# Block-sparse attention with a top-1 mixture of experts: exponentials, turned copies and gathered tokens in another order

## Chip, cores and metric

The kernel runs on one core of a Trainium2 chip. The metric is device time in microseconds (us), the median of several executions; lower is better. TensorE (PE, with its weight loads PEld), VectorE (DVE), ScalarE (ACT), GpSimd (POOL) and SyncE (SP, which here only issues DMAs) each run a queue of their own.

## The reference

```python
def _attn_ref(q, k, v, sampled_blocks):            # B=4, H=8, S=768, D=64
    scores = np.matmul(q, k.transpose(0, 1, 3, 2)) / np.sqrt(D)
    # blocks of 32: own block and both neighbours, the first and the last block
    # for all (their rows and their columns), 3 sampled blocks for each query block
    scores = np.where(mask, scores, -1000000000.0)
    attn = np.exp(scores - np.max(scores, axis=-1, keepdims=True))
    attn = attn / (np.sum(attn, axis=-1, keepdims=True) + 1e-09)
    return np.matmul(attn, v)

def _moe_ref(x, w_gate, w_output_gate, w1, w2):    # x: 3072 tokens x 512, 8 experts, FF 1024
    logits = x @ w_gate
    e_idx = np.argmax(logits, axis=1)
    gate_w = softmax(logits)[np.arange(N), e_idx]
    eom = 1.0 / (1.0 + np.exp(-(x @ w_output_gate)))
    for e in range(E):
        mask = e_idx == e
        h = np.maximum(x[mask] @ w1[e], 0.0)
        out[mask] = gate_w[mask, None] * eom[mask, e, None] * (h @ w2[e])
```

The tokens x are the attention's output, with the heads side by side.

## The kernel before

**Attention.** The work is cut into 52 pieces in a fixed order, and the loop at L1231 to L1265 runs one step for each, with three pieces in flight: in step n the scores of piece n (`now.pS`), the transposes of piece n-1 (`last.pT`) and the product with the values of piece n-2 (`before.pO`). The heads and batches form two groups (`bp`), and each has first four `Dense` pieces (query blocks 0 and 23, which see all 768 keys) and then 22 `Sparse` ones. So steps 0 to 3 and 26 to 29 make dense scores, and steps 1 to 4 and 27 to 30 turn the dense exponentials.

A dense piece does this: `pS` (L530) makes the scores in sixteen matmuls, which alternate between the two score banks S; `dM` (L538) takes the two maxima mx0d and mx1d on VectorE; `aE` (L546) makes four tiles of exponentials on ScalarE, P00d and P01d from the first bank, P10d and P11d from the second; `pT` (L553) turns each of the four by three transposes on TensorE (`turned`, L430, tiles T0d to T3d, for which there are two buffers) and copies the result out, T0d and T1d on ScalarE (L433), T2d and T3d on VectorE (L435); `pO` (L563) multiplies by the values, and `fin` (L442 to L444) divides. The next piece's scores overwrite both score banks, so they need the exponentials of the piece before.

In the program, in a step whose last piece is dense, `before.pO`, `last.pT(0)`, `now.dM` and `last.pT(1)` come first, and `now.aE` later, behind the work of other parts that the step holds (`mixed`, `run`). Each engine takes its instructions in the order in which the program records them.

**Experts.** Tokens are routed while the attention goes on (`route_a` to `route_d`; a scatter for each group of token tiles at the steps in SCATTER; `choose` picks five early units of work, u = 0 to 4, as soon as a group of tokens is known), and the rest is planned from step 26 + 31 on (`plan`). A unit is one expert with up to 256 tokens, and it is worked off in eight main steps, one for each piece of 512 KB of the expert's weights. FIRST = 31: main step 0 is step 31 of the loop. For each piece: `load_w` (L897, on SP), the high half of the weights in f16 on ScalarE (`w_h`, L976), the low half on VectorE (`w_l`, L980), twelve matmuls `p_h` (L994), relu into two halves (`h_h` L1007, `h_l` L1013) and the second product `p_y` (L1026); at the unit's end the scaled output (`y_o`, L1037) and its scatter to the result in HBM (`store_y`, L1044, on POOL).

The tokens of a unit come in four operations: `load_t` (L889, SP: the unit's part of the table of token numbers), `load_x` (L918, POOL: gathers of 128 tokens), `x_s` (L928 on ScalarE and L929 on VectorE: high and low half) and `x_t` (L943, DMA transposes on SP, for units from 6 on; units up to 5 are transposed by TensorE, L948, with a copy by ScalarE, L949). The planner (`program`, L1155) gives each operation a main step and a rank; `t = 8 * u` is the step of the unit's first piece.

Of the kernel before, what the change touches and what calls it, by code (L numbers as in the profile page):

```python
# [33 lines left out]
NE = 5  # L34
# [14 lines left out]


EARLY = {1: (0,), 2: (1, 2), 3: (3,), 4: (4,)}
EARLY_T = 27, 36, 38, 47, 52
EARLY_X = (28, 29), (37, 37), (39, 40), (48, 49), (53, 54)

SCATTER = {0: (18, 19, 20, 21), 1: (26, 26, 27, 27), 2: (34, 34, 35, 36), 3: (44, 45, 46, 47), 4: (50, 51, 52)}
OF = {u: g for g, us in EARLY.items() for u in us}

SX = 64.0
# [8 lines left out]
FIRST = PER + ND + 1  # L67
# [7 lines left out]
PEX = tuple(range(NE + 1))  # L75
# [21 lines left out]
def tile_kernel(ctx, tc, q, k, v, sampled, wg, wcat, out):  # L97
# [416 lines left out]
    class Dense:  # L514
# [34 lines left out]
        def pT(self, b):  # L549
            if b == 0:  # L550
                self.t = []
            for n in (2 * b, 2 * b + 1):
                self.t.append(turned(f"{n}" + self.name, self.p[n], 384, ("act", "dve")[b]))  # L553

        def pO(self):
            bp, u = self.k
# [505 lines left out]
    def at(n, rank, f, *a):  # L1062

        hooks.setdefault((n, rank), []).append((f, a))
# [31 lines left out]
    for bp in range(2):  # L1096
# [18 lines left out]
        for n, i in enumerate(tiles):  # L1115
# [7 lines left out]
            for g, (a, e) in enumerate(RG):  # L1123
                if e == tt + 1:
# [17 lines left out]
                    if g in EARLY:  # L1142
# [4 lines left out]
                        for u in EARLY[g]:  # L1147
                            at(t0 + 6, 3, load_r, u)
                            at(EARLY_T[u], 3, load_t, u)
                            for m in range(2):  # L1150
                                at(EARLY_X[u][m], 3, load_x, 2 * u + m)

    done = set()

    def program(n0, n1):  # L1155

        prog = {}

        def do(step, rank, f, a):
            u = NFC if f in (load_w, w_h, w_l, p_h, p_y) else NFC // 2 if f in (h_h, h_l) else 2 if f in (x_t, x_l, load_x, store_y) else 1  # L1160
            if n0 * u <= a < n1 * u and (f, a) not in done:
                done.add((f, a))
                prog.setdefault(step, []).append((rank, len(prog[step]) if step in prog else 0, f, a))

        for i in range(len(PLAN[1])):
            do(PLAN[0] + i, 11.5, plan, i)
        end = PLAN[0] + len(PLAN[1])
        for u in range(NUNIT):
            t = 8 * u
            yl = 2 if u < NOWN else 4  # L1170
            if u >= NE:
                later = end + u - NE
                do(max(t - 26, later), 0, load_g, u)
                do(max(t - 18, later), 0.5, load_t, u)
                for m in range(2):
                    do(max(t - 13, later + 1), 1, load_x, 2 * u + m)
                do(max(t - 7, later + 2), 13, x_s, u)
            for m in range(2):
                x = max(t - 2 + m, EARLY_X[u][m] + 1 - FIRST) if u < NE else t - 2 if u in PEX else t - 5
                do(x, 15, x_t, 2 * u + m)  # L1180
                do(x + 1 if u < NE else x, 3 if u < NE else 16, x_l, 2 * u + m)
            do(t + 8 + yl, 4 if u < NOWN else 12, y_o, u)
            for m in range(2):
                do(t + 8 + yl + 1 + (m if u < NOWN else 0), 13, store_y, 2 * u + m)
        for n in range(NP):
            e = n < NFC * NOWN
            lead, yl = (2, 2) if e else (3, 4)
            do(n - lead, 6, w_h, n)
            do(n - lead, 7, w_l, n)
            u, j = n // 8, n % 8  # L1190
            if e:

                do(max(n - 5, (-3, 5, 5, 15)[u]), 0.6, load_w, n)
            elif u < NE:
                do(n - 10, 0.6, load_w, n)
            else:
                do(max(n - 24 - lead + 1, end + u - NE, (30 + j // 2, 34 + j // 2)[u - NE] if u < NE + 2 else 0), 0.6, load_w, n)
            do(n, 8, p_h, n)
            do(n + yl, 9, p_y, n)
            if n % 2 == 1:  # L1200
                do(n if e else n + 1, 10, h_h, n // 2)
                do(n + 1, 2 if e else 11, h_l, n // 2)
        return prog
# [27 lines left out]
    for step in range(max(s for s, _ in hooks) + 1):  # L1231
        cur[0] = step
        now, last, before = unit(step), unit(step - 1), unit(step - 2)
        if now:
            now.pS()

        if isinstance(last, Dense):
            if before:
                before.pO()
            last.pT(0)  # L1240
            now.dM()
            last.pT(1)
        mixed(step, 0, 7)
        run(step, 0)
        if before and not isinstance(last, Dense):
            before.pO()
        if now and not isinstance(last, Dense):
            now.dM()
        run(step, 1)
        if before:  # L1250
            before.fin()

        if isinstance(now, Dense):
            now.aE()
        run(step, 2)
        mixed(step, 7, 9)
        if isinstance(now, Sparse) and step >= ONE_S:
            now.aE()
        if isinstance(last, Sparse):
            last.pT()  # L1260
        if isinstance(now, Sparse) and step < ONE_S:
            now.aE()
        mixed(step, 9, 99)
        for rank in (3, 4, 5):
            run(step, rank)  # L1265
# [64 lines left out]
```

## Time and profile before

| | |
|---|---|
| three executions | 608.76, 610.13, 615.25 us; median 610.13 |
| the profiled execution | 613.64 us, of it 611.8 in the span that the trace covers |
| mean granted clock of TensorE | 0.957 |
| busy share: PE, PEld, DVE, ACT, POOL | 89%, 62%, 63%, 56%, 38% |
| DMA | 136.28 MB, mean 223 GB/s |

A busy time is summed over the span, so it hides that the stages have different limits: the dense steps lie at 10 to 37 us and at 140 to 183 us, the sparse steps between and behind them, and expert work alone from about 320 us. A matmul line of the trace stands for a group of matmuls; "[0.41 <-ACT P01d L546]" at a line's end is the time that the engine was idle before it, and what ended it. [...]

### The profile page before, as it was taken

What the parts mean: (1) busy time and instruction counts of PE and PEld (TensorE: products, weight loads), DVE (VectorE), ACT (ScalarE), POOL (GpSimd) and SP (SyncE); (2) the same over time, 40 slices, a digit from 0 to 9 for tenths busy, and PEclk for the clock granted to TensorE, in tenths of its full rate; (3) what the DMA queues carried; (4) which work ended last, traced back from release to release, by engine and by line L of the source; (5) the groups of instructions that cost most, each with busy time, mean ns of one, the idle gap of its engine ahead of it and who ended that gap; (6) DMA issues with size and microseconds to landing.
All of it is one profiled execution on the core that took longest, in us unless ns stands there. A gap on an engine that the chain in (4) does not pass through costs nothing. (4 is left out here: it accounts for less than half of the span.)

```text
span 611.8 us, 18428 instructions
## 1 busy us (share of the span) xinstructions
PE 545.7 (89%) x7213; PEld 377.0 (62%) x7213; DVE 384.0 (63%) x753; ACT 343.2 (56%) x618; POOL 232.7 (38%) x347
## 2 busy tenths in 40 slices
PE   5799889998779997999999898894999999999994
PEld 3466666665457665667767666562666666666762
DVE  4567586575467665767745585674378657766960
ACT  1446465565356665666664464562458558656751
POOL 4944543826702848258471164001213131131101
PEclk7799898999889999999999999997899999999998
DMA  8959997971965579758763767999979859932200
GB/s 311 286 158 309 277 277 229 278 256 45 271 211 157 160 268 288 228 181 249 240 196 104 279 257 226 409 418 242 330 261 287 193 141 318 315 106 53 65 1 31
DMA packets 63839, 136.28 MB, mean 223 GB/s; under 512 B 25856, under 2 KB 32512, under 8 KB 63489
## 3 DMA queue, kind: packets, MB, share of 16 engines
q1 hardware_dynamic: 52160, 97.76, 51.1%
q0 software_dynamic: 11584, 37.27, 19.9%
q8 instruction: 59, 0.97, 0.6%
q14 instruction: 36, 0.29, 0.1%
HBM read 124.64 MB, written 15.60 MB: 229 GB/s over the span
## 5 line engine op out<-in xcount | busy, mean ns | idle before, releaser
L994 PE MATMUL h<-xb,kr 128*128 128x256 f16 (+1 forms) x1044 | 111.7, 257 | 12.7 <-DMA xb<-xb 9.0
L994 PEld LDWEIGHTS <-kr 128*128 128x128 f16 x1044 | 90.8, 98 | 41.4 <-issue 12.5
L1026 PE MATMUL S<-kr,hh 128*128 128x512 f16 x438 | 109.4, 382 | 0.0
L481 ACT ACTIVATE P<-S,mx 128x256 f32<-128x256 f32 x176 | 69.2, 482 | 10.4 <-DVE mx L473 10.4
L397 POOL TENSOR_TENSOR kr<-kn,eighth 128x256 f32<-128x256 f32 x110 | 67.6, 642 | 16.5 <-issue 8.0
L473 DVE TENSOR_REDUCE mx<-S 128x4 f32<-128x1024 f32 x44 | 53.7, 1221 | 31.9 <-PE S L466 18.8
L918 POOL DMA_INDIRECT xb<-xscr,tab x20 | 23.0, 1151 | 120.9 <-DMA tab<-table 32.8
L1026 PEld LDWEIGHTS <-hh 128*128 128x128 f16 x480 | 45.9, 98 | 37.0 <-issue 1.1
L1007 ACT ACTIVATE hh<-h 128x512 f16<-128x512 f32 (+1 forms) x48 | 25.2, 526 | 71.7 <-PE h L994 71.7
L980 DVE SCALAR_TENSOR_TENSOR kr<-e,kr 128x1024 f16<-128x1024 f32 x43 | 51.3, 1222 | 15.1 <-ACT kr L976 14.8
L433 ACT COPY pt<-T 128x512 f32<-128x512 f32 x66 | 36.6, 589 | 41.8 <-PE T L430 40.9
L414 POOL DMA_INDIRECT vt<-in_v_dram,vidx x44 | 47.2, 1072 | 28.3 <-PE O L499 22.2
L1013 DVE SCALAR_TENSOR_TENSOR hh<-h,hh 128x512 f16<-128x512 f32 (+1 forms) x48 | 28.7, 597 | 42.2 <-ACT hh L1007 42.2
L1044 POOL DMA_INDIRECT out_dram<-yo,tab x20 | 21.9, 1093 | 86.8 <-ACT yo L1037 78.5
L466 PE MATMUL S<-kr,qall 64*32 64x256 f32 x1408 | 52.2, 394 | 0.8 <-issue 0.4
L430 PE MATMUL T<-ident,P 128*128 128x128 f32 x352 | 48.1, 280 | 1.0 <-issue 0.5
L976 ACT ACTIVATE kr<-e 128x1024 f16<-128x1024 f32 x43 | 43.7, 1053 | 0.0
L430 PEld LDWEIGHTS T<-ident,P 128*128 128x128 f32 x352 | 41.3, 146 | 2.3 <-DVE lsum L624 1.0
L499 PE MATMUL O<-vt,pt 128*32 128x65 f32 x1408 | 34.2, 223 | 8.0 <-issue 7.6
L742 POOL DMA_INDIRECT table<-vals,place x24 | 26.3, 1094 | 31.5 <-DVE vals L691 14.9
L506 PE MATMUL O<-vc,pt 128*64 128x65 f32 x704 | 32.8, 229 | 5.7 <-issue 5.7
L499 PEld LDWEIGHTS O<-vt,pt 128*32 128x32 f32 x1408 | 26.3, 110 | 17.5 <-issue 14.5
(300 smaller groups left out, 944.4 us busy)
## 6 DMA issues: line engine op xcount, KB each, us to landing
e<-in_wcat_dram SPq DMA_DIRECT2D x80, 512.0 KB
rk<-in_wcat_dram SPq DMA_DIRECT2D x24, 512.0 KB
vn<-in_v_dram SPq DMA_DIRECT2D x12, 520.0 KB
qall<-in_q_dram SPq DMA_DIRECT2D x24, 256.0 KB
xscr<-x SPq DMA_DIRECT2D x48, 128.0 KB
vc<-in_wcat_dram SPq DMA_DIRECT2D x12, 512.0 KB
vc<-in_v_dram SPq DMA_DIRECT2D x22, 260.0 KB
ws<-in_wcat_dram SPq DMA_DIRECT2D x8, 512.0 KB
```

The costliest lines, as they stand in the source:

```text
L397: nc.gpsimd.tensor_tensor(r[:, slot], kn[bp][:, ds(rv, 1)].rearrange("p o n -> p (o n)"), eighth.to_broadcast([128, 256]), op=ALU.mult)
L414: nc.gpsimd.indirect_dma_start(vt[bp, i][:, s].rearrange("p b j w -> p (b j w)"), None, v, bass.IndirectOffsetOnAxis(ap=vidx[:, bp, i, s:s ...
L430: nc.tensor.transpose(pt[:, 128 * c:128 * c + 128], p[:, 128 * c:128 * c + 128], ident)
L433: nc.scalar.copy(t[:, 0:w], pt[:, 0:w])
L466: nc.tensor.matmul(s[64 * h2 + 32 * qi:64 * h2 + 32 * qi + 32, b, hp], t[p, 64 * j + 32 * qi:64 * j + 32 * qi + 32], g[p, 1 - qi:3:1 + qi, ...
L473: nc.vector.tensor_reduce(mx, self.s.rearrange("p b h n -> p (b h) n"), axis=AX.X, op=ALU.max, negate=True)
L481: nc.scalar.activation(p[:, 256 * hp:256 * hp + 256], self.s[:, b, hp], AF.Exp, bias=self.mx[:, 2 * b + hp:2 * b + hp + 1])
L499: nc.tensor.matmul(o[row:row + 32, b, hp, 0:VW], self.t[b][:, col:col + 32], av[:, qi, b, 4 * h2 + 2 * hg + hp], start=b == 0 and hp == 0, ...
L976: nc.scalar.activation(w[:, 0], piece(n), AF.Copy, scale=SW)
L980: nc.vector.scalar_tensor_tensor(w[:, 1], piece(n), SW, w[:, 0], op0=ALU.mult, op1=ALU.subtract)
L994: nc.tensor.matmul(hps[n // 2][:, cols(n)], w[:, hl, 128 * c:128 * c + 128], x[:, xl, c], start=cnt == 0, stop=cnt == 11)
L1026: nc.tensor.matmul(y, a[:, k], w[:, l, 512:1024], start=n % 8 == 0 and cnt == 0, stop=n % 8 == 7 and cnt == 2)
```

## The change

It has three parts.

1. In dense pieces VectorE copies the turned T0d and T1d, and ScalarE T2d and T3d; before it was the other way round. In a step whose last piece is dense, the maxima `now.dM` come ahead of `last.pT(0)`, and, where the step's own piece is dense too, its exponentials `now.aE` come between the two calls of `last.pT`, ahead of all that other parts of the program do in the step.
2. The scatters of token group 2 and the table loads and gathers of early units 1 and 2 each move one or two steps forward.
3. For planned units (u from 5 on) the table load moves two main steps forward, the gathers, the split `x_s` and the DMA transposes three.

```diff
-EARLY_T = 27, 36, 38, 47, 52
-EARLY_X = (28, 29), (37, 37), (39, 40), (48, 49), (53, 54)
+EARLY_T = 27, 35, 37, 47, 52
+EARLY_X = (28, 29), (36, 36), (38, 39), (48, 49), (53, 54)
-SCATTER = {..., 2: (34, 34, 35, 36), ...}
+SCATTER = {..., 2: (33, 33, 34, 34), ...}
...
     def pT(self, b):                                # Dense
-                self.t.append(turned(f"{n}" + self.name, self.p[n], 384, ("act", "dve")[b]))
+                self.t.append(turned(f"{n}" + self.name, self.p[n], 384, ("dve", "act")[b]))
...
     def program(n0, n1):
-                do(max(t - 18, later), 0.5, load_t, u)
+                do(max(t - 20, later), 0.5, load_t, u)
                 for m in range(2):
-                    do(max(t - 13, later + 1), 1, load_x, 2 * u + m)
-                do(max(t - 7, later + 2), 13, x_s, u)
+                    do(max(t - 16, later + 1), 1, load_x, 2 * u + m)
+                do(max(t - 10, later + 3), 13, x_s, u)
             for m in range(2):
-                x = ... if u < NE else t - 2 if u in PEX else t - 5
+                x = ... if u < NE else t - 2 if u in PEX else t - 8
...
         if isinstance(last, Dense):
             if before:
                 before.pO()
+            now.dM()
             last.pT(0)
-            now.dM()
+            if isinstance(now, Dense):
+                now.aE()
             last.pT(1)
...
-        if isinstance(now, Dense):
+        if isinstance(now, Dense) and not isinstance(last, Dense):
             now.aE()
```

ScalarE in step 28, before. The copies pt0d and pt1d belong to the piece of step 27, the exponentials P00d to P11d to that of step 28; xT is the routing's copy.

```order
L433 COPY pt0d_1_3339<-T0d_1_3335 128x384
L433 COPY pt1d_1_3345<-T1d_1_3341 128x384
L602 COPY xT_3367<-xp_3368 128x512
L546 ACTIVATE P00d_2_3379<-S_75,mx0d_2_3347 128x384
L546 ACTIVATE P01d_2_3381<-S_75,mx0d_2_3347 128x384
L546 ACTIVATE P10d_2_3383<-S_76,mx1d_2_3349 128x384
L546 ACTIVATE P11d_2_3385<-S_76,mx1d_2_3349 128x384
```

ScalarE in the same step, now.

```order
L546 ACTIVATE P00d_2_3351<-S_75,mx0d_2_3335 128x384
L546 ACTIVATE P01d_2_3353<-S_75,mx0d_2_3335 128x384
L546 ACTIVATE P10d_2_3355<-S_76,mx1d_2_3337 128x384
L546 ACTIVATE P11d_2_3357<-S_76,mx1d_2_3337 128x384
L433 COPY pt2d_1_3363<-T2d_1_3359 128x384
L433 COPY pt3d_1_3369<-T3d_1_3365 128x384
L602 COPY xT_3375<-xp_3376 128x512
```

The exponentials stand ahead of the copies and of the routing's copy. The same holds in steps 1 to 3 and 27 to 29.

ScalarE in step 29 and the start of step 30, before. Here ws is a conversion of expert weights (`w_h`), lt a copy of the routing's logits, and P_1_0_0 the exponentials of the first sparse piece, in step 30.

```order
L433 COPY pt0d_2_3467<-T0d_2_3463 128x384
L433 COPY pt1d_2_3473<-T1d_2_3469 128x384
L976 ACTIVATE ws_3492<-e_3363 128x1024
L618 COPY lt_3501<-lp_3496 128x128
L546 ACTIVATE P00d_3_3507<-S_75,mx0d_3_3475 128x384
...
L433 COPY pt0d_3_3614<-T0d_3_3610 128x384
L433 COPY pt1d_3_3620<-T1d_3_3616 128x384
L976 ACTIVATE ws_3493<-e_3363 128x1024
L481 ACTIVATE P_1_0_0_3644<-S_75,mx_0_0_3622 128x256 x2
```

The same stretch, now.

```order
L546 ACTIVATE P11d_3_3485<-S_76,mx1d_3_3465 128x384
L433 COPY pt2d_2_3491<-T2d_2_3487 128x384
L433 COPY pt3d_2_3497<-T3d_2_3493 128x384
L976 ACTIVATE ws_3500<-e_3371 128x1024
L618 COPY lt_3509<-lp_3504 128x128
...
L433 COPY pt2d_3_3628<-T2d_3_3624 128x384
L433 COPY pt3d_3_3634<-T3d_3_3630 128x384
L976 ACTIVATE ws_3501<-e_3371 128x1024
L481 ACTIVATE P_1_0_0_3644<-S_75,mx_0_0_3610 128x256 x2
```

The logits' copy, and in step 30 the sparse exponentials, keep their place behind the copies and the conversion, but these copies are now of T2d and T3d, which TensorE makes last.

SyncE around the transposes of unit 6 (xb), before. The other rows are weight pieces (`load_w`), into buffers e, vc and qall, and the table part of unit 7 (tab).

```order
L897 DMA e_3363<-in_wcat_dram 128x1024
...
L897 DMA vc_185<-in_wcat_dram 128x1024
L943 DMA_TRANSPOSE xb_6819<-xb_6818 128x8x128 x2
...
L897 DMA qall<-in_wcat_dram 128x1024
```

SyncE at the same place, now.

```order
L943 DMA_TRANSPOSE xb_6819<-xb_6818 128x8x128 x2
...
L897 DMA e_3371<-in_wcat_dram 128x1024
...
L897 DMA e_3371<-in_wcat_dram 128x1024
...
L897 DMA vc_185<-in_wcat_dram 128x1024
L889 ISA
L889 DMA tab_7696<-table 128x32
...
L897 DMA qall<-in_wcat_dram 128x1024
```

The transposes have passed three weight pieces, two into e and one into vc. The row of tab behind vc is a later unit's table part (unit 8), which stood further down.

## Rows read from the trace of the kernel before

**Rows 1.** Windows; columns: us, busy us (instructions) of PE, PEld, DVE, ACT, POOL, clock, DMA share, GB/s.

```profile
44.00:90.00 46.00, 40.23 (x963) 30.40 (x957) 33.02 (x82) 27.35 (x68) 23.14 (x33) 0.96 0.94 280
140.00:190.00 50.00, 40.50 (x560) 26.32 (x560) 27.58 (x64) 23.66 (x52) 19.73 (x27) 0.86 0.59 175
390.00:440.00 50.00, 39.57 (x255) 25.70 (x253) 24.09 (x25) 21.33 (x27) 6.19 (x5) 0.90 1.04 342
440.00:490.00 50.00, 49.33 (x389) 33.73 (x388) 36.36 (x39) 33.87 (x43) 10.68 (x10) 1.00 0.87 255
```

**Rows 2.** Timeline, steps 2 and 3; columns: start us, us, engine, line, instruction [idle before, releaser].

```profile
24.05 2.46 PE L530 MATMUL S<-kn,qall 64*64 64x384 f32 x16 [0.41 <-ACT P01d L546]
...
26.61 0.96 DVE L538 TENSOR_REDUCE mx0d<-S 128x1 f32<-128x768 f32 x1 [1.44 <-issue]
...
27.19 0.52 PE L563 MATMUL O<-vn,pt2d 128*64 128x65 f32 x12
27.48 0.95 DVE L538 TENSOR_REDUCE mx1d<-S 128x1 f32<-128x768 f32 x1
...
29.05 0.48 ACT L433 COPY pt0d<-T0d 128x384 f32<-128x384 f32 x1 [3.81 <-PE T1d L430]
...
29.59 0.55 PE L430 MATMUL T2d<-ident,P10d 128*128 128x128 f32 x3 [0.72 <-ACT pt0d L433]
29.80 0.60 ACT L546 ACTIVATE P00d<-S,mx0d 128x384 f32<-128x384 f32 x1
...
30.92 2.46 PE L530 MATMUL S<-kn,qall 64*64 64x384 f32 x16 [0.40 <-ACT P01d L546]
```

**Rows 3.** Timeline, steps 27 to 29, and a window of the same stretch (columns as in rows 1).

```profile
146.97 1.52 PE L530 MATMUL S<-kn,qall 64*64 64x384 f32 x16
...
153.43 2.46 PE L530 MATMUL S<-kn,qall 64*64 64x384 f32 x16 [0.56 <-ACT P01d L546]
...
156.00 0.96 DVE L538 TENSOR_REDUCE mx0d<-S 128x1 f32<-128x768 f32 x1 [1.21 <-PE S L530]
...
162.17 0.59 ACT L546 ACTIVATE P00d<-S,mx0d 128x384 f32<-128x384 f32 x1
...
163.28 3.77 PE L530 MATMUL S<-kn,qall 64*64 64x384 f32 x16 [1.63 <-ACT P01d L546]
166.99 0.92 PE L563 MATMUL O<-vn,pt0d 128*64 128x65 f32 x12
...
163.00:169.00 6.00, 5.72 (x54) 3.31 (x56) 1.82 (x2) 1.17 (x3) 2.12 (x3) 0.50 1.04 259
```

**Rows 4.** Timeline, steps 29 and 30.

```profile
171.06 1.07 ACT L976 ACTIVATE ws<-e 128x1024 f16<-128x1024 f32 x1
...
172.85 0.40 PE L623 MATMUL lp<-fold,lt 128*128 128x16 f32 x2 [0.38 <-ACT lt L618]
...
179.58 1.56 ACT L481 ACTIVATE P<-S,mx 128x256 f32<-128x256 f32 x4
```

**Rows 5.** Timeline around the first piece of unit 6 (SPq is SP's queue of DMA issues).

```profile
403.57 4.81 SPq L897 DMA_DIRECT2D e<-in_wcat_dram  x5
...
410.53 8.43 SPq L943 DMA_TRANSPOSE xb<-xb  x2
...
415.30 0.99 POOL L1044 DMA_INDIRECT out_dram<-yo,tab  x1 [0.30 <-issue]
416.34 1.46 PE L1026 MATMUL S<-kr,hh 128*128 128x512 f16 x6
...
426.70 0.34 SPq L889 DMA_DIRECT2D tab<-table  x1
426.81 2.72 PE L994 MATMUL h<-xb,kr 128*128 128x256 f16 x12 [9.01 <-DMA xb<-xb]
...
429.32 2.76 PE L1026 MATMUL S<-kr,hh 128*128 128x512 f16 x6
```

**Rows 6.** Waits of SP's queue; columns: who waited <- for what: us in total, times, longest.

```profile
SPq L889 <- DMA out_dram<-yo,tab: 24.7, 6, 7.4
```

More of the change, by code (lines that the diff above doesn't have):

```diff
@@ L51 @@
 EARLY = {1: (0,), 2: (1, 2), 3: (3,), 4: (4,)}
-EARLY_T = 27, 36, 38, 47, 52
-EARLY_X = (28, 29), (37, 37), (39, 40), (48, 49), (53, 54)
-SCATTER = {0: (18, 19, 20, 21), 1: (26, 26, 27, 27), 2: (34, 34, 35, 36), 3: (44, 45, 46, 47), 4: (50, 51, 52)}
+EARLY_T = 27, 35, 37, 47, 52
+EARLY_X = (28, 29), (36, 36), (38, 39), (48, 49), (53, 54)
+SCATTER = {0: (18, 19, 20, 21), 1: (26, 26, 27, 27), 2: (33, 33, 34, 34), 3: (44, 45, 46, 47), 4: (50, 51, 52)}
 OF = {u: g for g, us in EARLY.items() for u in us}
@@ L1173, in program @@
                 do(max(t - 26, later), 0, load_g, u)
-                do(max(t - 18, later), 0.5, load_t, u)
+                do(max(t - 20, later), 0.5, load_t, u)
                 for m in range(2):
-                    do(max(t - 13, later + 1), 1, load_x, 2 * u + m)
-                do(max(t - 7, later + 2), 13, x_s, u)
+                    do(max(t - 16, later + 1), 1, load_x, 2 * u + m)
+                do(max(t - 10, later + 3), 13, x_s, u)
             for m in range(2):
-                x = max(t - 2 + m, EARLY_X[u][m] + 1 - FIRST) if u < NE else t - 2 if u in PEX else t - 5
+                x = max(t - 2 + m, EARLY_X[u][m] + 1 - FIRST) if u < NE else t - 2 if u in PEX else t - 8
                 do(x, 15, x_t, 2 * u + m)
```

## The prediction

> **What bounds the kernel now.** I read the page first for the stages, then windows of 40 to 50 us, then the timeline wherever a window shows TensorE short of work. TensorE is the busiest engine, and two stretches decide [rows 1]. From 440 us on it is busy for 49.33 of 50 us at clock 1.00: there no edit to another engine gains anything, and whatever is won earlier arrives at the end undiminished, as long as the weights keep up. In 140 to 190 it is busy for only 40.50 of 50 at a mean clock of 0.86, and in 390 to 440 for 39.57 of 50 at 0.90. The change touches the cause of each: the second group of dense steps lies in the first window, the first planned unit with DMA transposes (unit 6) in the second. The first group of dense steps ends at 37 us; behind it, in 44 to 90, the DMA share is 0.94, so a gain made there can be lost again to loads.
>
> In a dense step the chain is scores, maximum, exponentials, next scores. In step 3 the first maximum is ready at 27.57 and the second at 28.43, but the first exponential starts at 29.80 [rows 2]: ScalarE had stood idle for 3.81 us and then copied pt0d and pt1d, because its queue holds them ahead. The next scores start at 30.92, released by P01d, and take 2.46 us where an undisturbed set takes 1.52 [rows 2, 3]: half of them wait for the second bank. In step 28 it is worse [rows 3]. [...]
>
> Before unit 6 TensorE ends its last product at 417.80 and starts at 426.81, after 9.01 us of waiting for the transposed tokens [rows 5]. After the hole it runs one `p_h` and one `p_y` at half rate: 2.76 us where 1.46 was the time before, so 1.3 each, some 2.7 in all.
>
> **Part 1, first dense group (steps 1 to 4).** Each step loses no instruction; the order changes. Take step 3: the exponentials run from 27.7 to about 29.7 (four of 0.60 that overlap a little). VectorE does both maxima first and copies T0d and T1d from 28.5 to 29.55 (0.5 each). TensorE's T2d must wait for the first of these copies as it now waits for ScalarE's, until about 29.05, and T3d ends near 30.15. The next scores start there, not at 30.92, a gain of 0.77, and take 1.52, not 2.46, a gain of 0.94: 1.7 in this step. In step 2 the same gain of 0.94 is mostly paid for: T0d's copy now stands behind both maxima, which are late there, so I let the scores start 0.65 later than the 24.05 of now; net 0.3. For step 4, where the sparse scores wait for the last dense exponentials, I take 0.4. Sum 2.4. At the bounds it is 0 (swallowed by the loads behind, DMA share 0.94 [rows 1]) and 3.5 (two steps like step 3). I take 2.4, because the scores of the first sparse steps are started by TensorE's progress and not by a load.
>
> **Part 1, second dense group (steps 27 to 30).** In step 27 the scores of step 28 shrink from 2.46 to 1.52: 0.94. In step 28 the exponentials no longer wait for the routing's copy; the wait of 1.63 goes, and the scores go from 3.77 to 1.52, another 2.25, of which 0.94 is the wait for the second bank and the rest the half clock. The four groups of `pO` behind them (166.99 and following, 0.92 the first) take 0.52 each at full clock [rows 2]; of 4 x 0.40 I count 1.2, since the groups overlap. Sum 6.0, if the clock stays up when TensorE no longer pauses. Against it stand two losses. In step 29 the logits' copy lt now follows pt2d, pt3d and a conversion ws of 1.07 us [rows 4], with TensorE's next matmul L623 waiting directly for it: about 1.0. In step 30 the sparse exponentials, which start at 179.58, come behind the copies of T2d and T3d, which TensorE can make only when VectorE has copied T0d and T1d behind the maximum: about 1.5 for the scores of step 31. Net 3.5. The bounds are a gain of 7.2 (no losses, and 1.2 of half clock saved in one more `pO`) and a loss of 0.6 (the clock falls as before, which leaves 6.0 - 1.3 - 1.2 = 3.5, and the losses are 4.1, not 2.5). I take 3.5, the sum of the rows one by one.
>
> **Part 3, the tokens of unit 6.** The two transposes were issued from 410.53, behind five pieces of e and one of vc that take (410.53 - 403.57) / 6 = 1.16 us each [rows 5]. They now pass three of these, so they are issued 3 x 1.16 = 3.5 us earlier; the three pieces follow them, and by the planner the weights are asked for more than 20 pieces ahead, so nobody waits for those. If they land as much earlier, the hole shrinks from 9.0 to 5.5. A hole of 5.5 is still one in which I expect the clock to fall, so the 2.7 behind it stay. Gain 3.5; bounds 0 (they land when they land now) and 9.0 + 2.7 = 11.7 (hole closed, clock kept). For the later units nothing is to be won, as TensorE has no gap there.
>
> A row speaks against this term: SP's table load, released at 426.70, waited for scatters of the result (out_dram), the second of which POOL issued at 415.30 only, and TensorE was released 0.11 us later, at 426.81, by the transposes [rows 5]. Both may have ended with the same traffic. [...] Against it, transposes that are issued 3.5 us earlier have fewer scatters ahead of them, and POOL's gather for unit 7, behind which the scatters stand, comes earlier too, as its table part moves ahead of six loads.
>
> **Part 2** I take at nothing. What moves is POOL's scatters and gathers and two table parts of SP's queue in steps 33 to 40, one or two steps each, under the sparse steps that TensorE fills as it does those of 44 to 90 (40.23 of 46 [rows 1]); their lead over their users hides them. Without that cover a step's delay would cost 1 us or so either way, which lies inside the range.
>
> **Sum.** 2.4 + 3.5 + 3.5 = 9.4. The profiled execution took 613.64 (span 611.8 and 1.84 around it) and would take 604.2; the median of 610.13, 3.5 below it, becomes 600.7, 1.5% less. About 1%, or 604.0 to 616.2, is what a measurement of this kernel can tell from no change.
>
> **The rivals.**
>
> B, the hole closes: the transposes land with nothing in their way, and neither the 9.0 nor the half clock remains. 610.1 - 2.4 - 3.5 - 11.7 = 592.5. For it: the loads around 403 to 410 fill the DMA engines (share 1.04 in that window [rows 1]), and a transpose issued before three of them may land by more than their issue time earlier. Against: it must gain three times what the issue does.
>
> C, the transposes are held by the scatters, as in the row against: 610.1 - 5.9 = 604.2.
>
> D, the clock falls in steps 28 to 30 in spite of the shorter wait, since TensorE still waits for copies there, and the first group's gain is lost to the loads: the second group gives 3.5 less the 1.3 and 1.2 of half clock, 1.0, part 3 still 3.5: 605.6. For it: a mean clock of 0.86 over 50 us is 14 us at half clock, more than the 6 us of 163 to 169 [rows 1, 3], so there is another cause of it; against: the longest wait of these steps is the one that goes.
>
> E, slower: SP's queue blocks. The table load of a unit now stands two main steps earlier, but its releaser, the scatter of an earlier unit's result, stays where it is. SP already waits there six times, 24.7 us in all and 7.4 at the longest [rows 6], with all weight loads behind it. A main step is one `p_h` and one `p_y`; at half clock their starts lie 2.51 apart (429.32 - 426.81), so a whole step at full clock is about 2.5, and the wait may grow by 5.0 for each unit. The DMA share of 0.87 leaves 13% of a unit's 20 us, 2.6, to catch up. What is left, 2.4 for each of the units 6 to 15, is 24, and with the gain of 9.4 that gives 624.7. It decides only once the lead of 20 pieces, 50 us, is used up; 24 us do not use it up, which is the reason against.
>
> **How the numbers follow.** The forecast (600.7, by itself 597 to 604) has 0.45, B 0.15, C 0.15, D 0.16, E 0.05, and 0.04 is left for what I don't see. Faster by over 1% are nearly all of the forecast (0.42), B, and less than half of C (0.06): 0.63. Within 1%: D, the rest of C, the forecast's edge and half of what is left, 0.30. Slower: E and the other half, 0.07. The range from 592 to 608 reaches from B to beyond D and covers the bounds of each term taken one at a time; E stands outside.
>
> **What would show it.** Right: in steps 1 to 3 and 27 to 29 the first exponential starts within 0.3 us of its maximum's end, and all dense scores take about 1.5 us with no wait on ScalarE of over 0.5; the window that answers to 163 to 169 shows clock 1.00; L623 waits some 1 us longer for lt; TensorE's wait for xb before unit 6 is 5 to 6 us and the clock falls behind it. Wrong: a wait for xb of 9 us (C) or none (B), half clock in steps 28 to 30 (D), or SP's waits for out_dram well over 24.7 us with TensorE waiting for weights behind them (E).

## The result

| | before | changed |
|---|---|---|
| median of 20 executions, us | 610.44 | 607.31 |
| lowest and highest | 606.31, 615.75 | 597.02, 615.41 |
| the profiled execution, span | 613.64, 611.8 | 602.52, 600.7 |
| mean granted clock | 0.957 | 0.967 |

The ratio is 0.987, with a 95% interval of 0.982 to 0.992. The comparison leaves out executions more than 1.5% above the fastest of their kernel, which keeps 6 of the changed kernel's 20 and 19 of the other's, so the ratio shows a larger gain than the medians of all 20, which differ by 3.1 us or 0.5%. The change is a gain, of 0.5 to 1.3% by these two readings; the profiled pair, 11.1 us apart, overstates it.

### The profile page after: what moved, and what is told of

Read it like the earlier page. It is cut to its first block, busy times and chain, and to the rows that moved or that the text cites. A ratio compares the mean times of both kernels' runs of the same rounds, so it can differ in the third digit from the quotient of the medians.

```text
span 600.7 us, 18428 instructions
## 1 busy us (share of the span) xinstructions
PE 539.4 (90%) x7213; PEld 374.2 (62%) x7213; DVE 385.8 (64%) x753; ACT 344.8 (57%) x618; POOL 232.6 (39%) x347
## 5 line engine op out<-in xcount | busy, mean ns | idle before, releaser
L994 PEld LDWEIGHTS <-kr 128*128 128x128 f16 x1044 | 90.8, 98 | 35.7 <-ACT kr L976 5.9
L397 POOL TENSOR_TENSOR kr<-kn,eighth 128x256 f32<-128x256 f32 x110 | 68.1, 646 | 15.4 <-issue 9.0
L1007 ACT ACTIVATE hh<-h 128x512 f16<-128x512 f32 (+1 forms) x48 | 25.3, 527 | 70.7 <-PE h L994 70.6
L499 PEld LDWEIGHTS O<-vt,pt 128*32 128x32 f32 x1408 | 27.1, 111 | 18.4 <-issue 15.1
L742 POOL DMA_INDIRECT table<-vals,place x24 | 26.9, 1119 | 29.8 <-DVE vals L691 15.1
```

The lines of the kernel that those rows point to most:

```text
L397: nc.gpsimd.tensor_tensor(r[:, slot], kn[bp][:, ds(rv, 1)].rearrange("p o n -> p (o n)"), eighth.to_broadcast([128, 256]), op=ALU.mult)
L499: nc.tensor.matmul(o[row:row + 32, b, hp, 0:VW], self.t[b][:, col:col + 32], av[:, qi, b, 4 * h2 + 2 * hg + hp], start=b == 0 and hp == 0, ...
L994: nc.tensor.matmul(hps[n // 2][:, cols(n)], w[:, hl, 128 * c:128 * c + 128], x[:, xl, c], start=cnt == 0, stop=cnt == 11)
```

## The profile after, beside the rows of before

Windows of the changed kernel that answer to [rows 1], the later ones taken 4 us earlier; columns as there. The clock is the one granted to TensorE, as a share of its full speed, so that 0.50 is half clock.

```profile
44.00:90.00 46.00, 40.47 (x986) 30.01 (x983) 32.35 (x85) 28.52 (x73) 24.37 (x35) 1.00 1.00 309
136.00:186.00 50.00, 40.38 (x607) 26.33 (x609) 29.17 (x66) 26.06 (x56) 19.69 (x27) 0.86 0.65 187
386.00:436.00 50.00, 47.49 (x331) 32.22 (x330) 31.53 (x33) 27.78 (x36) 8.05 (x7) 1.00 1.02 357
436.00:486.00 50.00, 46.15 (x355) 31.21 (x354) 31.59 (x33) 29.12 (x39) 8.81 (x9) 0.97 0.92 255
```

The third window has won 8 us of TensorE's time and full clock. The fourth, which had nothing to win, has lost 3. In the second TensorE is busy no longer than before, although it gets through more (607 instructions for 560): one wait went and another came.

The first dense group, step 2, timeline of the changed kernel; it answers to [rows 2].

```profile
26.37 0.96 DVE L538 TENSOR_REDUCE mx0d<-S 128x1 f32<-128x768 f32 x1 [1.18 <-ACT kr L395]
...
27.36 0.58 ACT L546 ACTIVATE P00d<-S,mx0d 128x384 f32<-128x384 f32 x1 [1.16 <-DVE mx0d L538]
...
28.32 0.56 DVE L435 COPY pt0d<-T0d 128x384 f32<-128x384 f32 x1
...
28.94 0.55 PE L430 MATMUL T2d<-ident,P10d 128*128 128x128 f32 x3 [0.32 <-issue]
...
29.88 1.52 PE L530 MATMUL S<-kn,qall 64*64 64x384 f32 x16
```

The first exponential starts 0.03 us after its maximum, VectorE copies T0d while ScalarE is at work, and the next scores take 1.52 us without a wait.

The second group, steps 28 and 29, timeline, and behind it the window that answers to 163 to 169 in [rows 3].

```profile
152.48 0.58 ACT L546 ACTIVATE P00d<-S,mx0d 128x384 f32<-128x384 f32 x1 [2.31 <-DVE kr L405]
...
155.16 0.56 DVE L435 COPY pt0d<-T0d 128x384 f32<-128x384 f32 x1 [1.85 <-remote]
155.49 0.58 ACT L546 ACTIVATE P10d<-S,mx1d 128x384 f32<-128x384 f32 x1 [1.95 <-remote]
...
155.77 0.55 PE L430 MATMUL T2d<-ident,P10d 128*128 128x128 f32 x3 [2.17 <-DVE pt0d L435]
...
157.55 1.52 PE L530 MATMUL S<-kn,qall 64*64 64x384 f32 x16
159.00 0.57 PE L563 MATMUL O<-vn,pt0d 128*64 128x65 f32 x12
```

```profile
157.00:163.00 6.00, 5.52 (x84) 3.72 (x87) 3.37 (x7) 3.56 (x8) 4.75 (x7) 1.00 1.02 252
```

The scores of step 29 have lost their wait of 1.63 us and run at clock 1.00. TensorE's 2.17 us before T2d are a wait that neither the kernel before (0.29 us at this place) nor part 1 alone (0.32) has; VectorE and ScalarE stood still at the same time (more under the table of the experiments). In the second trace of the changed kernel ("changed, once more" among the experiments) the same wait is 2.03 us, and there the clock does fall behind it; the scores of step 29 take 2.19 us:

```profile
160.00:162.00 2.00, 2.00 (x11) 1.20 (x13) 0.22 (x1) 1.27 (x3) 1.98 (x4) 0.50 1.01 210
```

Steps 29 to 31; they answer to [rows 4].

```profile
163.27 1.06 ACT L976 ACTIVATE ws<-e 128x1024 f16<-128x1024 f32 x1
...
164.54 0.40 PE L623 MATMUL lp<-fold,lt 128*128 128x16 f32 x2 [1.15 <-ACT lt L618]
...
165.71 1.96 PE L466 MATMUL S<-kr,qall 64*32 64x256 f32 x32
...
174.43 1.56 ACT L481 ACTIVATE P<-S,mx 128x256 f32<-128x256 f32 x4
...
176.05 1.96 PE L466 MATMUL S<-kr,qall 64*32 64x256 f32 x32 [2.36 <-ACT P L481]
177.94 0.92 PE L563 MATMUL O<-vn,pt0d 128*64 128x65 f32 x12
```

The scores of steps 30 and 31 in the kernel before:

```profile
173.86 1.10 PE L466 MATMUL S<-kr,qall 64*32 64x256 f32 x32
...
182.57 1.96 PE L466 MATMUL S<-kr,qall 64*32 64x256 f32 x32
```

Here is the new wait: the scores of step 31 stand 2.36 us for the sparse exponentials of step 30, where they had no wait before. They then run at half clock (0.50 from 176 to 182; 1.96 us, where those of step 32 take 1.09), but so they did in this trace of the kernel before (0.50 from 182.5 to 186.5). New, too, is the half clock in step 30, behind L623's wait of 1.15 us: 0.50 from 165.5 to 167.7, and 1.96 us for scores that took 1.10, at 1.00 from 173 to 175.

SP, POOL and TensorE around units 6 and 8, timeline, and behind it the waits of SP's table loads; they answer to [rows 5, 6].

```profile
402.94 9.31 SPq L943 DMA_TRANSPOSE xb<-xb  x2
...
406.77 0.99 POOL L1044 DMA_INDIRECT out_dram<-yo,tab  x1 [0.30 <-ACT kr L976]
...
415.21 0.33 SPq L889 DMA_DIRECT2D tab<-table  x1
...
415.99 1.47 PE L994 MATMUL h<-xb,kr 128*128 128x256 f16 x12 [1.09 <-DMA xb<-xb]
...
428.88 1.00 POOL L1044 DMA_INDIRECT out_dram<-yo,tab  x1 [0.30 <-ACT kr L976]
...
435.67 0.33 SPq L889 DMA_DIRECT2D tab<-table  x1
...
442.25 7.04 SPq L943 DMA_TRANSPOSE xb<-xb  x2
...
447.17 0.99 POOL L1044 DMA_INDIRECT out_dram<-yo,tab  x1 [0.30 <-ACT kr L976]
...
453.83 0.33 SPq L889 DMA_DIRECT2D tab<-table  x1
453.97 1.74 PE L994 MATMUL h<-xb,kr 128*128 128x256 f16 x12 [3.85 <-DMA xb<-xb]
```

```profile
SPq L889 <- DMA out_dram<-yo,tab: 32.3, 7, 9.6
```

The wait before unit 6 is 1.09 us where it was 9.01, and the clock did not fall behind it (1.00 from 416 to 422, where it was 0.50 from 426.8 to 432). A wait of 3.85 before unit 8 is new. Ahead of it SP stood at a table load until 435.67, that is 6.8 us after the second scatter of an earlier unit, with five weight pieces and unit 8's transposes queued behind.

## The experiments

Each set of runs has executions of the kernel before on the same chip. Two of the sets ran on two other chips, on which the kernel before takes 594 to 598 us, not 610 to 613, so that only ratios go from one set to another, and even they then compare different chips. From chips of 610 to 613 us come the rows "before" (both), "changed" (both), "late tables" and "copies not swapped"; the others come from the faster two. The reading used for the dense steps is the distance between starts of scores:

| us | step 1 to 4 | 27 to 30 | 30 to 32 |
|---|---|---|---|
| before | 20.1 | 26.9 | 15.4 |
| before, six tables | 19.6 | 26.6 | 13.7 |
| tokens alone | 19.7 | 26.5 | 13.7 |
| early alone | 19.7 | 25.3 | 13.7 |
| changed | 17.6 | 22.4 | 17.9 |
| changed, once more | 17.6 | 23.5 | 17.8 |
| dense alone | 17.5 | 20.4 | 17.4 |
| changed, six tables | 18.2 | 20.4 | 17.0 |
| changed, late tables | 18.4 | 23.1 | 17.0 |
| changed, six tables, late scatters | 19.0 | 20.4 | 16.6 |
| changed, six tables, exponentials first | 17.6 | 20.4 | 14.6 |
| changed, copies not swapped | 19.1 | 23.5 | 15.3 |
| changed, exponentials not moved | 27.1 | 28.1 | 16.7 |

Two differences in the table are not plainly the edit's. The wait before T2d in step 28 is there in all four traces with the moved exponentials from chips of 610 to 613 us (1.86 to 2.17 us) and in none of the five from the faster chips, so the gain from 27 to 30 is some 2 us smaller on the former; whether the change brings this wait about there stays open. And from 30 to 32 the first row is 1.7 us above the other three that have these steps as before, since in that trace alone the scores of step 31 ran at half clock (1.96 us, not 1.09).

### The three parts by themselves

Part 1 alone is the kernel before with the two edits of the dense steps:

```diff
+            now.dM()
             last.pT(0)
-            now.dM()
+            if isinstance(now, Dense):
+                now.aE()
             last.pT(1)
...
-            ... ("act", "dve")[b]
+            ... ("dve", "act")[b]
```

> The kernel before with part 1 alone (dense steps). Theory: part 1 is worth what the lead of the changed kernel over the kernel before shows at the start of step 33, 5.6 us (2.2 from the first dense group, 3.4 from the second), and the wait of 9 us before unit 6 stays: about 604.5 us, ratio 0.991. In the trace the dense scores take 1.5 us each, and step 33 starts near 183.6, not 189.3. Rival: the lead of the dense steps is used up by the load-bound sparse steps and by waits in the experts, so that less than 2 us arrive: 608 to 610, ratio 0.997 or more.

Ratio 0.994 (0.991 to 0.998); medians 592.96 and 597.70. In the table, step 1 to 4 loses 2.2 us, 27 to 30 loses 5 to 6, and 30 to 32 takes 3.7 longer than in the two other parts by themselves on this chip. The wait before unit 6 is there, 8.6 us. (The start named as step 33's in the expectation is that of step 32.) The medians are 4.7 us apart, so most of the lead of the dense steps arrives.

Part 3 alone:

```diff
-                do(max(t - 18, later), 0.5, load_t, u)
+                do(max(t - 20, later), 0.5, load_t, u)
-                    do(max(t - 13, later + 1), 1, load_x, 2 * u + m)
+                    do(max(t - 16, later + 1), 1, load_x, 2 * u + m)
-                do(max(t - 7, later + 2), 13, x_s, u)
+                do(max(t - 10, later + 3), 13, x_s, u)
-                x = ... else t - 5
+                x = ... else t - 8
```

> The kernel before with part 3 alone (table, gathers, split and transposes of planned units moved forward). Theory: the wait for the tokens before unit 6 falls from 9 to 1 or 2 us and the half clock behind it goes, but a new wait of about 4 us opens before unit 8, because SP's queue stands at a table load until scatters of the result have landed: net gain 4 to 8 us, 602 to 606 us, ratio 0.987 to 0.993. Rival: the two waits cancel, or the wait before unit 6 only moves: 609 to 611.

Ratio 0.992 (0.988 to 0.996). The wait before unit 6 is 3.45 us, not the 1 or 2 expected, and one of 4.85 us stands before unit 8. Both halves of the theory are there without the dense edits. The traced execution took 598.74 us, more than the median of the kernel before. In it unit 8 takes back what unit 6 wins, 6.4 us each by the starts of the pieces against those of part 1 alone, which is the rival's picture; the gain in the ratio is that of other executions.

Part 2 alone:

```diff
-EARLY_T = 27, 36, 38, 47, 52
-EARLY_X = (28, 29), (37, 37), (39, 40), (48, 49), (53, 54)
+EARLY_T = 27, 35, 37, 47, 52
+EARLY_X = (28, 29), (36, 36), (38, 39), (48, 49), (53, 54)
-SCATTER = {..., 2: (34, 34, 35, 36), ...}
+SCATTER = {..., 2: (33, 33, 34, 34), ...}
```

> The kernel before with part 2 alone (scatters of token group 2, tables and gathers of units 1 and 2). Theory: nothing, ratio 0.998 to 1.002, since all of it lies under steps that TensorE fills. Rival: 2 us either way, since the scatters stand in POOL's queue among gathers of values.

Ratio 0.995 (0.991 to 0.999): not nothing. The waits of TensorE in 200 to 260 us say where it comes from. First the kernel before, then part 1 alone; in part 2 alone and in the changed kernel there is no such row.

```profile
PE xgp L948 <- DMA e<-xscr,tab: 2.1, 1, 2.1
```

```profile
PE xgp L948 <- DMA e<-xscr,tab: 2.6, 2, 2.2
```

TensorE had stood 2.1 us for the gathered tokens of an early unit, and with one step's lead no trace shows that wait. But the kernel before with six tables (below) has no such row either, without the lead, so that the wait is not in every execution, and that the gain of part 2 is this wait is likely and not shown. (The trace of part 2 alone keeps the hole before unit 6, 8.60 us.)

The changed kernel itself, in the next set:

> The changed kernel itself once more, beside the next three on one chip. Theory: the three parts alone gave 0.9943, 0.9923 and 0.9947; if they add up, the whole gives 0.981. Rival: they overlap (the experts' waits for tokens take back what the steps before them win), and the whole gives 0.987 or more.

Ratio 0.990 (0.983 to 0.997), medians 608.45 and 612.59. The three ratios multiply to 0.981, below both measurements of the whole (0.987 and 0.990), so the rival's reading is the nearer one: the parts seem not to add up in full. It is not settled. The product of the three has an interval of its own, about 0.975 to 0.988 (an estimate from the three), which overlaps with that of the whole, and the whole did not run on the chip of the parts.

### Which half of part 1 does it

The copies as before, all else as in the changed kernel:

```diff
-... ("dve", "act")[b]
+... ("act", "dve")[b]
```

> The changed kernel with the copies of the turned tiles back as before (T0d and T1d on ScalarE, T2d and T3d on VectorE); the exponentials then stand behind the copies of T0d and T1d, but still ahead of the routing's copy and the weights' conversion. Theory: in steps 2 and 3 of the first dense group all is as before (scores of 2.46 us, 2 us of lead lost at step 5), while in step 28 most of the gain stays, since there the exponentials had waited for the routing's copy: scores of step 29 without the wait of 1.6 us and at clock 1.00. 1 to 3 us slower than the changed kernel. Rival: without the swap the second group falls back, too, with a wait of over 1.3 us before the scores of step 29: 5 us slower.

Ratio 0.981 (0.975 to 0.987), the interval overlapping that of the changed kernel; the medians, 608.21 and 608.45 for the changed kernel in the same set, are alike. The table has the theory's picture: step 1 to 4 goes back to 19.1, while 27 to 30 keeps most of its gain (23.5, as in the changed kernel of this set); the scores of step 29 have no wait, but take 2.00 us. The 1 to 3 us by which the kernel should be slower are not there. And 30 to 32 is 15.3, 2.5 us less than with the swap. So the swap pays in the first group and costs in step 30, where T2d and T3d, the last to be turned, stand ahead of the sparse exponentials.

The other half, the swap with the exponentials back behind the other work:

```diff
-            if isinstance(now, Dense):
-                now.aE()
             last.pT(1)
...
-        if isinstance(now, Dense) and not isinstance(last, Dense):
+        if isinstance(now, Dense):
             now.aE()
```

> The changed kernel with the exponentials back behind the other work of the step; the maxima still stand first and the copies stay swapped (T0d and T1d on VectorE). Theory: the gain of the dense steps needs the exponentials ahead of ScalarE's copies; without it T2d's copy by ScalarE comes after both pairs of transposes and the exponentials after that, so the dense scores wait for P01d again by 1 us or more and the first group loses its lead (step 4 starts 19.5 us or more after step 1, against 17.8 in the changed kernel). Rival: the swap alone keeps most of it, 18.3 us or less.

One execution, 607.26 us where the kernel before has 594.27. Step 1 to 4 takes 27.1 us, over 7 more than without any of it. In the timeline:

```profile
24.03 0.48 ACT L433 COPY pt2d<-T2d 128x384 f32<-128x384 f32 x1 [5.93 <-PE T2d L430]
24.49 0.48 ACT L433 COPY pt3d<-T3d 128x384 f32<-128x384 f32 x1
24.87 0.59 ACT L546 ACTIVATE P00d<-S,mx0d 128x384 f32<-128x384 f32 x1
...
25.98 3.71 PE L530 MATMUL S<-kn,qall 64*64 64x384 f32 x16 [1.52 <-ACT P01d L546]
```

All four tiles must now be turned before ScalarE comes to an exponential. The scores wait 1.52, 1.58 and 1.62 us in steps 2 to 4 (for the third the profile names no releaser), the dense ones take 3.71 and 3.41 us, and the mean clock from 24 to 46 is 0.84. So the swap gains only together with the order of the exponentials. In the second group that order alone carries the gain (23.5 with and without the swap); in the first it needs the swap, by which VectorE does the early copies beside the exponentials (17.6 with it, 19.1 without, 19.6 to 20.1 before).

### Why a wait opens before unit 8

A table buffer is used again four units on, and the scatter of the unit that had it reads its token numbers from it: SP's table loads wait for scatters to out_dram, 32.3 us in all in the changed kernel. Two more buffers:

```diff
-... tag="tab", name=f"tab{u}", bufs=4)
+... tag="tab", name=f"tab{u}", bufs=6)
```

> The changed kernel with six table buffers where it has four, so that a unit's table load no longer waits for the scatter of the unit four before. Theory (SP's queue is blocked at the table load): SP's waits for out_dram ahead of table loads go from 32 us to under 5, the transposes of unit 8 are issued earlier, and its wait of 3.9 us and the half clock behind it go: 4 to 6 us below the changed kernel, ratio 0.975 to 0.98. Rival (the transposes' completion is held by the scatters in flight, whatever SP does): the waits of SP go, but TensorE's wait before unit 8 stays at 3 us or more, and the time is that of the changed kernel, ratio about 0.987.

Ratio 0.975 (0.970 to 0.981), clear of the changed kernel's two intervals, which are from other chips; some of the distance can be the chip's, as the wait in step 28 shows. SP no longer waits for out_dram at any table load (32.3 us in the changed kernel), and there is no wait before unit 8. SP's queue shows why; unit 8's transposes are the second row:

```profile
386.51 10.35 SPq L943 DMA_TRANSPOSE xb<-xb  x2
...
422.22 6.00 SPq L943 DMA_TRANSPOSE xb<-xb  x2
```

Unit 8's come 35.7 us behind unit 6's; in the changed kernel it is 39.3 (402.94 to 442.25). The wait before unit 6 is 3.53 us here. Over all traces with the tokens moved forward by the change's steps the picture is the same: with four tables TensorE waits 1.4 to 4.9 us before unit 8 in six of six (in the shortest the profile names ScalarE as the releaser), with six tables not at all in two of two, and 5.41 us where the scatters, too, are moved (below). With the tokens where they were, only part 2 alone has such a wait, of 2.04 us.

The same two buffers in the kernel before:

> The kernel before with six table buffers where it has four and nothing else changed. Theory: the extra buffers gain only because the change moved the table loads ahead of the scatters; in the kernel before, SP's waits for out_dram (25 us) mostly lie where the weights are far ahead, so the wait of 9 us before unit 6 stays and the time moves by less than 2 us, ratio 0.997 to 1.0. Rival: the blocked queue bounds the kernel before, too, and the ratio is 0.99 or below.

Ratio 0.997 (0.992 to 1.001). SP's waits (24.7 us) go here, too, and the wait before unit 6 stays:

```profile
PE h L994 <- DMA xb<-xb: 8.3, 1, 8.3
```

So here the buffers paid only with the tokens moved (0.975, and 0.997 without): the planner of before loads a table one step behind the scatter that frees its buffer, the change puts it one step ahead.

The table loads back, without more buffers:

```diff
-                do(max(t - 20, later), 0.5, load_t, u)
+                do(max(t - 18, later), 0.5, load_t, u)
```

> The changed kernel with the table loads of planned units back at 18 steps ahead, where the kernel before has them; gathers, split and transposes stay three steps forward. Theory (SP's queue is blocked at the table load because it now stands ahead of the scatter that frees its buffer): SP's waits for out_dram fall from 32 us to 25 or less, the wait before unit 8 (3.9 us) goes, and the time is 3 to 5 us below the changed kernel. Rival: the wait before unit 8 is of the transposes' own making, stays at 3 us or more, and the time is that of the changed kernel.

Ratio 0.979 (0.973 to 0.985), medians 601.09 and 608.45 for the changed kernel. The time went as the theory had it, the trace did not: SP still waits 35.5 us for out_dram, 8.5 at the longest, and the wait before unit 8 is 4.66. So one step's order was not enough to free the queue. The time is then no evidence for the theory. Against the changed kernel's second trace 6.4 of 7.1 us are won from step 4 to 27 (105.9 us for 112.3), before the first of these table loads, so that most of it is not the edit's work in that pair; why the six executions are faster stays open.

### Whether the scatters hold the transposes

In the changed kernel both waits for transposes ended within 0.8 us of a release by the scatters (415.21 and 415.99, 453.83 and 453.97), as in [rows 5]. With six tables, unit 4's scatters four main steps later:

```diff
-            do(t + 8 + yl + 1 + (m if u < NOWN else 0), 13, store_y, 2 * u + m)
+            do(t + 8 + yl + 1 + (m if u < NOWN else 4), 13, store_y, 2 * u + m)
```

> The changed kernel with six table buffers and the scatters of results four main steps later, so that those of unit 4 are issued after the transposes of unit 6 and not among them. Theory A (the transposes' completion is held by the scatters issued meanwhile): the transposes are reported within 1 us of the end of their issue, and the wait before unit 6 falls from 3.5 to under 1 us. Theory B (the transposes are slow by themselves, among the weight loads that fill the DMA engines): the wait stays at 3 us or more.

One execution, 591.32 us where the kernel before has 594.27: little of what six tables won is left. Before unit 6, where no scatter is under way now, TensorE doesn't wait at all. The scatters have moved among unit 8's transposes, and there a wait has come, where six tables alone had none:

```profile
424.36 8.25 SPq L943 DMA_TRANSPOSE xb<-xb  x2
...
431.15 1.00 POOL L1044 DMA_INDIRECT out_dram<-yo,tab  x1 [0.31 <-ACT yo L1037]
...
440.81 2.72 PE L994 MATMUL h<-xb,kr 128*128 128x256 f16 x12 [5.41 <-DMA xb<-xb]
```

The transposes of unit 8 were reported 8.2 us after their issue ended (432.61), where unit 6's with scatters among them took 3.7 in the changed kernel. Both places agree with theory A, and neither settles it: gathers of tokens moved along with the scatters, and TensorE came to unit 6 late enough that a landing some 3 us after the end of the issue would not have shown.

### Further forward

Six tables, and in step 30 the sparse exponentials first:

```diff
-            if isinstance(now, Dense):
+            if isinstance(now, Dense) or step >= ONE_S:
                 now.aE()
             last.pT(1)
...
-        if isinstance(now, Sparse) and step >= ONE_S:
+        if isinstance(now, Sparse) and step >= ONE_S and not isinstance(last, Dense):
             now.aE()
```

> The changed kernel with six table buffers, and in step 30 the sparse exponentials also ahead of the copies of T2d and T3d and of the weights' conversion. Theory: the wait of 2.4 us for these exponentials before the scores of step 31, which the change has brought in, goes, and with it the half clock that follows in steps 31 and 32: 2 to 4 us below the kernel with six tables (ratio 0.975), so 0.97. Rival: the copies of T2d and T3d are then late for the product of step 31 and the conversion for its piece, the wait moves there, and the ratio is 0.975 or more.

Ratio 0.972 (0.967 to 0.978), medians 579.14 and 594.27. Step 30 to 32 falls from 17.0 to 14.6, and the scores of step 31 have neither a wait nor half clock:

```profile
169.87 1.57 ACT L481 ACTIVATE P<-S,mx 128x256 f32<-128x256 f32 x4 [2.27 <-DVE mx L473]
...
174.63 1.09 PE L466 MATMUL S<-kr,qall 64*32 64x256 f32 x32
```

The place of the loss is shown. In time the step from 0.975 is inside the intervals. It has the lowest ratio of the study.

The transposes ten steps ahead, in the same kernel:

```diff
-                x = ... else t - 8
+                x = ... else t - 10
```

> The kernel of the run before, with the DMA transposes ten steps ahead of their unit, not eight. Theory: they pass two more weight pieces, are issued 2 to 4 us earlier, and the wait before unit 6 (3.5 us with six tables) and the half clock behind it (2.6 us) go: 0.963 to 0.967. Rival: the transposes land only with the scatters of unit 4, as the coincidences in the traces suggest, whenever they are issued; the wait stays at 3 us or more.

This tells nothing of the question. There are two buffers for turned tokens, and ten steps ahead a unit's transposes overwrite those of the unit two before while its last piece has still to be multiplied; so this piece takes the wrong unit's tokens, and TensorE waits for them before the last piece of each of units 4 to 13:

```profile
PE h L994 <- DMA xb<-xb: 57.4, 10, 19.5
```

The ratio is 1.09. By the planner's order nine steps are as far as two buffers go, one more than the change takes; that was not run.

## Why the prediction was right, and where it was not

The direction held, and the range, by 0.7 us at its upper end; the forecast of 600.7 is near the ratio's 602, but its gain of 9.4 is twice to three times what the medians gained (3.1 and 4.1). That it is near the ratio is in part luck: of its terms only the first came out at its size, and the errors of the others pull both ways.

**First dense group: 2.4 predicted.** The profiled pair has 20.1 to 17.6, 2.5 us, and over the runs 19.6 to 20.1 became 17.5 to 18.4, with one 19.0. The mechanism is the one named, and it holds step by step: by the scores of steps 2, 3 and 4 the pair shows 0.5, 1.7 and 0.3 where 0.3, 1.7 and 0.4 were put. One sign failed: the scores of step 1 still wait 2.15 us and take 3.78, as before, since the piece ahead of them has no dense piece before it and its exponentials were not moved. Whether the gain is lost to the loads behind (D) the traces don't tell: from step 4 to 27 the kernel before takes 109.6 us, the changed kernel 108.1 and 112.3. The ratio of part 1 alone speaks against a loss.

**Second group, the gain of 6.0.** The wait and the wait for the second bank went, and in the pair the half clock with them, as the window at clock 1.00 shows; in the changed kernel's second trace half clock is still there at 160 to 162 us, which is D's sign, as is that of step 30 in the pair (below). Less the logits' copy, 5.0 were to be had by step 30. The pair has 4.5 (26.9 to 22.4), and the runs without the wait before T2d some 6 (to 20.4). L623's wait grew from 0.38 to 1.15, 0.8 where 1.0 was put. The half clock behind it, some 1.2 us in step 30 of the pair, was in no term; in part 1 alone the same wait of 1.15 us has none behind it (1.09 us for the scores). (The losses of 4.1 in the lower bound rest on no rows.)

**Second group, the loss in step 30: mis-sized.** The step was that the sparse exponentials come behind the copies of T2d and T3d, "about 1.5 for the scores of step 31". The pair shows 2.5, the other kernels with the swap, against the three rows of 13.7, 2.9 to 4.1 (16.6 to 17.8). The sum had priced the wait and not the half clock behind it. In the pair that half clock is only partly new, since the scores of step 31 ran at 1.96 us before, too; what is new is that it reaches further into step 31, for 0.9 us more up to step 32 (0.50 for 6 us, from 176 to 182, where it was 4, from 182.5 to 186.5), and the half clock of step 30 named above. Net 2.0 in the pair against 3.5.

**Unit 6: the wrong size, and a cost left out.** "A hole of 5.5 is still one in which I expect the clock to fall" did not come true: 1.09 us were left, the clock held (1.00 from 416 to 422), and 7.9 + 2.7 were won. Over all traces the wait is 8.3 to 9.0 us in the four kernels with the tokens where they were, and 0 to 3.5 in nine traces with them moved forward. So the term's size, three pieces' issue time, was wrong, and B's the nearer picture. But "for the later units nothing is to be won" was read as nothing to be lost, and E's mechanism took part of it back: SP's queue blocked at the table load, 9.6 us at the longest and 32.3 in all. It did not use up the weights, as E had it; it delayed the transposes that stand in the same queue, for 3.85 us before unit 8 and, over the next three groups of matmuls, about 1.8 of half clock behind it (0.50 from 456 to 458). Net about 5 in the pair, where 3.5 was forecast, as a gain three times the forecast's less a loss that it did not have.

**C** was half right. That the scatters hold the transposes, by which C has 5.9 = 2.4 + 3.5 and nothing for part 3, no run shows. What the traces show is that TensorE's release by the transposes follows SP's by the scatters by 0.78 and 0.14 us at the two waits of the changed kernel, where it was 0.11 before. This nearness did not keep the wait before unit 6 at 9 us: the scatters had moved too, to 406.77 from 415.30, as the prediction's reason against C had it.

**Part 2: failed.** "their lead over their users hides them" overlooked TensorE's 2.1 us for tokens of an early unit, which the waits of 200 to 260 us list. The term had been argued from the window of 44 to 90 us alone; part 2 by itself gave 0.995.

The terms of the profiled pair, 2.5 + 2.0 + 2.1 + 5, come near its 11.1, but the lead does not grow by them, so that this is luck. By the starts of the same matmuls in both traces the changed kernel leads by 2.2 us at step 4, 3.7 at step 27, 8.2 at step 30 and 5.6 at step 32, but by 2.9 ahead of unit 6, where part 2 should have added its 2.1; then by 13.5 behind the hole of unit 6, 8.2 behind that of unit 8 and 11.0 at the end. The dense steps and units 6 and 8 show as told; the rest comes and goes where no term has its place. From step 4 to 27, where the edits hardly reach, the traces take from 105 to 112 us. Nor does one pair explain medians only 3 to 4 us apart: a trace shows one execution, and the waits before units 6 and 8 differ from one to the next (1.1 and 3.9 us in one trace of the changed kernel; 2.7 and, for ScalarE, 1.4 in the other, which stands 2.1 us before unit 12 as well).

## What to carry to other kernels

When a load is moved forward, look at what frees its buffer. Here that release came later than the new place, SP's queue stood at the table loads for 32.3 us in all and 9.6 at the longest, and with two more buffers these waits and the 3.85 us before unit 8 were gone. When copies are swapped between two engines, follow the group to its last step: here the sparse exponentials stood behind the copies there, and the scores of step 31 waited 2.36 us. And list the waits of every stretch that an edit touches before pricing it at nothing: here one of 2.1 us was in the list, and the part gave 0.995.

## What was not expected of the hardware

- TensorE stands still for 1 us or more at several places of the attention steps, at some of them with VectorE and ScalarE all but idle beside it: for 2.49 us up to 92.98 in the kernel before (VectorE busy for 0.27 us of it, ScalarE for 0.19), for 1.93 up to 87.41 in the changed one (0.39 and 0.15). Most places change from trace to trace: in the kernel of "Further forward" TensorE waits 4.48 us up to 91.66, in the middle of a product, in part 1 alone 2.56 us up to 69.79. One place does not change: in the changed kernel ScalarE (1.95 us), VectorE (1.85) and TensorE (2.17) stop near 153.3 in step 28, the profile names only a remote release for the first two, and all four traces with the moved exponentials from chips of 610 to 613 us have a wait there, none of those from the faster chips. No run tells the cause.
- Issuing two DMA transposes held SP's queue for 9.31 us at 402.94, 7.04 at 442.25 and 10.35 with six tables, where a table load takes 0.33.
- Transposes with scatters issued among them were reported 3.7 us (unit 6 of the changed kernel) and 8.2 us (unit 8 with late scatters) after the end of their issue. Whether the scatters hold them is not settled.
